# Moving the 80 KB load of the last 64 MLP units from the first to the last of four w_down loads

## The chip, the core and the metric

The kernel runs on one core of one Trainium2 chip. The metric is the device time of one execution in microseconds (us). Times of the trace are counted from the start of the profiled span, which begins after the execution does: a run of 205.6 us has a span of 203.8 us.

The engines are named as the profile does: PE is TensorE's matmul and PEld its weight load, DVE is VectorE, ACT ScalarE, POOL GpSimd, SPq the queue of SyncE, which issues the loads. The page counts 16 DMA engines, and each load of 128 rows leaves 16 increments of its semaphore in the trace (the "landings"), for the last load of before from 198.33 to 200.49 us. The load has *landed* with the sixteenth. The trace doesn't name the engine of an increment; below, each increment is read as one engine's share of the load having arrived, which is the author's reading.

## The reference

One decode step: layer norm, attention over a cache of 4,096 keys for 32 heads, a residual, layer norm, and a gated MLP with 1,728 hidden units. Only its last product matters here.

```python
def _B_ref(x, w_gate, w_up, w_down):        # x: 640, w_gate and w_up: 640 x 1728
    g = jnp.einsum("bsd,df->bsf", x, w_gate)
    u = jnp.einsum("bsd,df->bsf", x, w_up)
    h = _gelu(g) * u
    return jnp.einsum("bsf,fd->bsd", h, w_down)   # w_down: 1728 x 640
# ... attention left out
h2 = h + _B_ref(_layernorm(h), w_gate, w_up, w_down)
```

## The kernel before

Nearly everything that the kernel reads is read once, 84 MB, over one queue: wq, then K and V of eight groups of four heads, parts of wo between them, then w_gate, w_up and w_down. 1,728 hidden units are 13 columns of 128 (unit `p * 13 + c` is row p of column c) and 64 more. The 64 rows of w_down left over are loaded as 128 half rows of 320 values (640 bytes), so that they fill 128 partitions too. They make columns 13 and 14 of `hid`, the hidden units that w_down multiplies: one for the left halves and one for the right.

The loads of w_down wait for the buffer of a K tile, and there are four of them:

```python
WD = ((0, 8), (8, 11), (11, 13))       # columns of the three large loads
FULL, NFC, YR, YW = 13, 15, 4, 160
# ...
load("wg", wg_sb, ...)                 # w_gate, 2,160 KB
load("wu", wu_sb, ...)                 # w_up, 2,160 KB
SP.wait_ge(S["pe"], pe_at(NQ - SLOTS, ("s", 1)))
load("wd0", wd_last, B_w_down[FULL * P : DF, :].rearrange("i (b d) -> (i b) d", b=PER))   # 80 KB
wd_rows = B_w_down[0 : FULL * P, :].rearrange("(p c) d -> p c d", c=FULL)
for i, (a, b) in enumerate(WD):        # 1,280, 480 and 320 KB
    load(f"wd{i + 1}", wd_sb[:, a:b, :], wd_rows[:, a:b, :])
```

The output row of 640 values is kept as four rows of 160, one for each 32-column group of the array. A column of `hid` is the stationary operand, 128 x 1. So a column of w_down takes four matmuls, one in each column group, and these run side by side: in the trace of before, the last eight begin within 0.01 us of each other in each set of four, and the second set 0.07 us after the first (200.61 after 200.54 us). Below, such a set of four is called a *pass*. Columns 13 and 14 take two matmuls each and are one pass together.

```python
end("u", up(u_ps, wu_sb, "wu"))
fill(4)                                 # matmuls without use
PE.wait_ge(S["dve"], D_HID)             # hid is ready
down = {FULL: "wd0", 0: "wd1", WD[1][0]: "wd2", WD[2][0]: "wd3"}
order = [*range(WD[0][1]), *range(FULL, NFC), *range(WD[0][1], FULL)]
for c in order:
    if c in down:
        landed_once(down[c])            # PE waits for the load
    for r in range(YR):
        if c < FULL:
            w = wd_sb[:, c, r * YW : (r + 1) * YW]
        elif r // 2 == c - FULL:
            w = wd_last[:, (r % 2) * YW : (r % 2 + 1) * YW]
        else:
            continue
        inst = y_matmul(r, slice(0, YW), hid[:, c : c + 1], w, c == order[-1])
end("y", inst)
# ... VectorE waits for that, adds h_row and SyncE stores y_row
```

`hid` is the end of a chain through all engines: the last scores, Exp, P times V, the projection, layer norm, gate, gelu, up.

The softmax here doesn't subtract the row's maximum and nothing guards it: scores larger than these inputs give would overflow.

## Time and profile before

| | before |
|---|---|
| time, median of 3 runs | 205.67 us (205.64 to 205.74) |
| profiled run, span | 205.61 us, 203.8 us |
| DMA, mean over the span | 414 GB/s, 84.38 MB |
| last load of w_down landed | 200.49 us |
| VectorE's last addition began | 200.90 us |

The first view is the page of the kernel before. The two rows have a digit for each of 40 slices of the span: the busy share of the DMA engines in tenths, and what they moved.

```profile
DMA  7999999999999999999999999999999999999991
GB/s 249 402 468 418 389 482 412 415 434 444 447 404 414 447 421 424 431 431 450 418 424 416 452 424 431 444 437 424 424 431 437 412 418 457 431 404 429 430 388 47
```

The DMA engines are busy throughout, except in the first and the last slice. The next view is the end of the chain of waits that ended last, in order of time (start, duration, what).

```profile
167.43 33.07 DMA big<-in_B_w_down_dram
200.49 0.04 issue
200.54 0.34 PE tp_105 L455 x8
200.88 0.02 issue
200.90 0.33 DVE y_row L725
```

The last load, of columns 11 and 12, is issued at 167.4 and lands at 200.49 us, 33 us later; eight loads issued before it, 13.9 MB, land in that time. Eight matmuls follow, which are two passes, and VectorE starts 0.41 us after the landing. The timeline of the same stretch (start, duration, engine, line, operation; in brackets the idle time before it and what ended it) shows when TensorE could begin.

```profile
198.59 0.18 DVE L723 TENSOR_TENSOR hid<-g_sb,u_col 128x15 bf16<-128x15 f32 x1
198.83 0.58 PEld L455 LDWEIGHTS tp_105<-big,hid 128*1 128x1 bf16 x36 [0.54 <-DVE hid L723]
...
199.75 0.17 PEld L455 LDWEIGHTS tp_105<-big,hid 128*1 128x1 bf16 x12 [0.34 <-DMA big<-in_B_w_down_dram]
200.54 0.10 PEld L455 LDWEIGHTS tp_105<-big,hid 128*1 128x1 bf16 x8 [0.62 <-DMA big<-in_B_w_down_dram]
200.54 0.31 PE L455 MATMUL tp_105<-big,hid 128*1 128x160 bf16 x8 [0.41 <-DMA big<-in_B_w_down_dram]
200.90 0.33 DVE L725 TENSOR_TENSOR y_row<-tp_105,h_row 128x160 bf16<-128x160 f32 x1 [2.12 <-PE tp_105 L455]
```

The first 36 matmuls wait for `hid`, the last 20 for loads. In this trace the four loads land in the order of issue, at 195.45, 198.55, 199.71 and 200.49 us.

### The profile page before, as it was taken

How to read it: one execution, taken by the hardware profiler on the slowest of the kernel's cores; microseconds unless marked ns; L12 is line 12 of the kernel's file. 1: busy time of each engine (PE TensorE's matmuls, PEld its weight loads, DVE VectorE, ACT ScalarE, POOL GpSimd, SP SyncE). 2: the span in 40 equal slices, each digit the busy share in tenths (PEclk: the TensorE clock that was granted, in tenths of full speed). 3: DMA queues.
4: the chain of work that ended last, by engine and by line, in shares of the span. 5: the costliest groups of instructions: out<-in, count | busy, mean ns of one | idle time of the engine just before them, and what ended most of it. 6: DMA issues, size and time to landing. Idle time of an engine off the chain costs nothing. (4 is left out here: it accounts for less than half of the span.)

```text
span 203.8 us, 7455 instructions
## 1 busy us (share of the span) xinstructions
PE 149.6 (73%) x3451; PEld 136.6 (67%) x3453; DVE 70.6 (35%) x163; ACT 81.5 (40%) x179; POOL 20.3 (10%) x20
## 2 busy tenths in 40 slices
PE   0003679765995499849984998389839989988993
PEld 0001179665995499849974997389839989987431
DVE  4003138201560067005700670039005801842460
ACT  0000327530566047704770467028703862773000
POOL 8301000710000001700000017000000000000000
PEclk9999969955698569856985698569856985995799
DMA  7999999999999999999999999999999999999991
GB/s 249 402 468 418 389 482 412 415 434 444 447 404 414 447 421 424 431 431 450 418 424 416 452 424 431 444 437 424 424 431 437 412 418 457 431 404 429 430 388 47
DMA packets 4058, 84.38 MB, mean 414 GB/s; under 512 B 464, under 2 KB 592, under 8 KB 848
## 3 DMA queue, kind: packets, MB, share of 16 engines
q1 hardware_dynamic: 4048, 84.23, 96.9%
q8 instruction: 8, 0.13, 0.3%
q14 instruction: 2, 0.02, 0.0%
HBM read 84.23 MB, written 0.00 MB: 413 GB/s over the span
## 5 line engine op out<-in xcount | busy, mean ns | idle before, releaser
L281 PE MATMUL o<-ex,big 128*128 128x4 bf16 x1024 | 29.8, 166 | 10.9 <-ACT ex L611 6.5
L281 PEld LDWEIGHTS o<-ex,big 128*128 128x128 bf16 x1024 | 28.4, 103 | 12.2 <-ACT ex L611 7.7
L597 ACT COPY big<-tp_104 128x1024 bf16<-128x1024 bf16 x16 | 16.2, 1012 | 50.0 <-PE tp_104 L255 50.0
L255 PE MATMUL tp_103<-ident,big 128*128 128x128 bf16 x256 | 23.9, 249 | 13.6 <-PEq L180 13.6
L255 PEld LDWEIGHTS tp_103<-ident,big 128*128 128x128 bf16 x256 | 19.5, 115 | 14.0 <-issue 14.0
L624 DVE COPY big<-tp_103 128x1024 bf16<-128x1024 bf16 x24 | 16.5, 688 | 21.2 <-PE tp_103 L255 21.2
L255 PE MATMUL tp_104<-ident,big 128*128 128x128 bf16 x256 | 23.5, 245 | 0.0
L255 PE MATMUL tp_105<-ident,big 128*128 128x128 bf16 x256 | 23.1, 242 | 0.0
L542 POOL COPY wo<-wo_in 128x5120 bf16<-128x5120 bf16 x3 | 13.4, 4451 | 93.5 <-PE a L292 93.5
L255 PE MATMUL tp_106<-ident,big 128*128 128x128 bf16 x256 | 22.5, 239 | 0.0
L255 PEld LDWEIGHTS tp_104<-ident,big 128*128 128x128 bf16 x256 | 19.3, 113 | 0.0
L255 PEld LDWEIGHTS tp_105<-ident,big 128*128 128x128 bf16 x256 | 18.9, 111 | 0.0
L255 PEld LDWEIGHTS tp_106<-ident,big 128*128 128x128 bf16 x256 | 18.6, 109 | 0.0
L624 DVE COPY big<-tp_106 128x1024 bf16<-128x1024 bf16 x24 | 16.6, 691 | 2.9 <-PE tp_106 L255 2.4
L268 PE MATMUL sb<-q_78,big 128*128 128x4 bf16 x512 | 14.2, 164 | 4.5 <-issue 4.5
L597 ACT COPY big<-tp_105 128x1024 bf16<-128x1024 bf16 x16 | 16.2, 1014 | 2.6 <-PE tp_105 L255 2.5
L268 PEld LDWEIGHTS sb<-q_78,big 128*128 128x128 bf16 x512 | 13.6, 96 | 4.6 <-issue 4.6
L611 ACT ACTIVATE ex<-sa 32x64 bf16<-32x64 f32 x32 | 9.8, 307 | 11.4 <-PE sa L268 11.2
L624 DVE COPY big<-tp_105 128x1024 bf16<-128x1024 bf16 x16 | 11.1, 692 | 8.4 <-PE tp_105 L255 8.1
L268 PE MATMUL sa<-q_78,big 128*128 128x4 bf16 x512 | 14.0, 164 | 0.0
L268 PEld LDWEIGHTS sa<-q_78,big 128*128 128x128 bf16 x512 | 13.5, 96 | 0.6
L681 DVE COPY o_raw<-o 128x4 f32<-128x4 f32 x4 | 0.7, 163 | 36.1 <-PE o L281 36.1
(111 smaller groups left out, 115.8 us busy)
## 6 DMA issues: line engine op xcount, KB each, us to landing
big<-in_A_v_cache_dram SPq DMA_DIRECT2D x8, 4096.0 KB, 33.9
big<-in_A_k_cache_dram SPq DMA_DIRECT2D x7, 4096.0 KB, 27.4
big<-in_A_wq_dram SPq DMA_DIRECT2D x1, 5120.0 KB, 15.4
wo_in<-in_A_wo_dram SPq DMA_DIRECT2D x4, 1280.0 KB, 28.3
big<-in_A_k_cache_dram SPq DMA_DIRECT2D x2, 2048.0 KB, 24.3
big<-in_B_w_gate_dram SPq DMA_DIRECT2D x1, 2160.0 KB, 39.5
big<-in_B_w_up_dram SPq DMA_DIRECT2D x1, 2160.0 KB, 44.1
big<-in_B_w_down_dram SPq DMA_DIRECT2D x1, 1280.0 KB, 32.1
```

The source lines that it names most:

```text
L255: inst = PE.transpose(tp_b[g % NBANK][:, b * DH : (b + 1) * DH], kt[slot][:, g * GRP + b, :], ident[:])
L268: inst = PE.matmul(s_ps[half][:, j % (NB // 2), :], lhsT=kt[slot][:, j, :], rhs=q8[:, slot * QH : (slot + 1) * QH], start=True, stop=True,)
L281: inst = PE.matmul(o_ps, lhsT=vt[slot][:, j, :], rhs=e_t[:, j, :], start=(j == 0), stop=(j == NB - 1))
L542: POOL.tensor_copy(wo_t[:], wo_in[:]).then_inc(S["wo"], 1)
L597: ACT.copy(group(m % SLOTS, g), tp_g[g % NBANK]).then_inc(S["act_pe"], 1)
L611: inst = ACT.activation(e_t[r, cols, i], s_ps[half][r, :, i], AF.Exp, scale=SCALE, accum_out=rs_all[r, half, h : h + 1])
L624: DVE.tensor_copy(group(m % SLOTS, g), tp_g[g % NBANK]).then_inc(S["dve_pe"], 1)
L681: event(DVE.tensor_copy(o_raw[:, HG * turn : HG * turn + QH], o_ps))
```

## The change

The intent is to have as little as possible left to do when the last load lands. The total of the loads can't shrink, but the smallest of them, whose columns need only one pass, can come last.

```diff
-    order = [*range(WD[0][1]), *range(FULL, NFC), *range(WD[0][1], FULL)]
+    order = range(NFC)
...
-            inst = y_matmul(r, slice(0, YW), hid[:, c : c + 1], w, c == order[-1])
+            inst = y_matmul(r, slice(0, YW), hid[:, c : c + 1], w, c >= FULL)
...
-    load("wd0", wd_last, B_w_down[FULL * P : DF, :].rearrange("i (b d) -> (i b) d", b=PER))
     wd_rows = B_w_down[0 : FULL * P, :].rearrange("(p c) d -> p c d", c=FULL)
     for i, (a, b) in enumerate(WD):
         load(f"wd{i + 1}", wd_sb[:, a:b, :], wd_rows[:, a:b, :])
+    load("wd0", wd_last, B_w_down[FULL * P : DF, :].rearrange("i (b d) -> (i b) d", b=PER))
```

## The prediction

> **What bounds the kernel.** DMA. The page's slices show the DMA engines at 90% or more of every slice but the first and the last, 414 GB/s on average (84.38 MB in a span of 203.8 us). The chain of waits that ended last is a DMA from 167.43 to 200.49 us (w_down's columns 11 and 12, the last load), then 8 matmuls on the y bank (from 200.54), the final addition on VectorE at 200.90, and the store. The other engines are off this chain: `hid` is ready at 198.8, and TensorE then waits three times for w_down (y's weight loads 1.0 us in two waits, the matmuls 0.4 us).
>
> **What the change does.** It removes and adds no work: 84 MB, 56 down matmuls and four loads stay. It moves the 80 KB load (128 rows of 640 B) behind the other three. [...] the four loads land in the order of issue, at 195.45, 198.55, 199.70 and 200.49 us. The moved load's packets took 32 ns each (the last load's 2,560 B took 102), so with 8 on each engine it is about 0.26 us of each engine's queue; it landed 0.19 us after w_up. So I expect the three large loads 0.19 to 0.26 us earlier, at about 198.3, 199.5 and 200.3, and the small one last at about 200.49, unchanged, because every engine has the same packets to move in total. From the last packet's end to the landing is 0.44 us for the small load and for the large last one alike, so no gain or loss there.
>
> **What lies on the critical path.** Only what follows the last landing. Before, 8 matmuls (two columns times four column groups): VectorE starts 0.36 us after the first. After, 4 matmuls, one for each column group: one pass of the array instead of two. I estimate 0.08 us less (8 matmuls spanned 0.31 us, one alone 0.23). The earlier landings are worth nothing: columns 0 to 7 still wait for `hid` at 198.83, columns 8 to 10 then run at about 199.5 to 199.8, columns 11 and 12 start at about 200.3 and are through TensorE's queue before 200.5.
>
> **Predicted time.** 205.67 - 0.08 = 205.59 us; range 205.35 to 205.82, since the DMA engines finish up to 2.2 us apart (first and last engine of the last load: 198.33 and 200.49), and a stalled packet on the slowest (two of 3,840 B took 355 and 414 ns instead of 149) is larger than the effect. Faster by over 2%: 0.005; within 2%: 0.99; slower: 0.005.
>
> **What would show it.** Right: in the landings, the large loads 0.2 us earlier and the last one still 33 us after its issue; in the timeline, a last group of 4 y matmuls instead of 8, and VectorE 0.25 to 0.3 us after its start instead of 0.36; all before 198 us unchanged. Wrong step "same last landing": the small load lands later than 200.49 by more than 0.1 us. Wrong step "second pass": VectorE still starts 0.36 us after the last group's start.
>
> **What would make it wrong.** Small packets at the end of the queue may not overlap as they do amid large ones, so that the slowest engine ends later and the gain is lost or turned round (about +0.2 us); or the last loads may spread differently over the engines and end earlier or later together.

"8 on each engine" and "the same packets" for every engine are the author's estimate, from 128 packets of 640 bytes and 16 engines; the trace doesn't name the engine of a packet. Both traces have 4,048 packets in this queue. That small packets overlap amid large ones is read from the same numbers: eight of 32 ns are 0.26 us, and the load landed 0.19 us after w_up.

## The result

| | before | after |
|---|---|---|
| time, median of 6 runs each | 205.65 us (205.54 to 205.74) | 205.50 us (205.37 to 205.74) |
| ratio | | 0.9993, 95% interval 0.998 to 1.0006 |
| last load of w_down landed | 200.49 us | 200.51 us |
| `hid` written, start | 198.59 us | 199.31 us |
| VectorE's last addition began | 200.90 us | 200.84 us |

A ratio is the mean time of one kernel's runs over that of the other's of the same rounds, so it is not quite the ratio of the medians in the table. Executions over 1.5% slower than the fastest of the same kernel are left out of the means. The interval holds 1: the time is the same within what six runs can tell, and the median lies in the predicted range.

The landings of the profile after are 198.34, 199.51, 200.30 and 200.51 us: the large loads 0.2 us earlier, the last one where it was. The timeline of the kernel after, for the same stretch as shown of before:

```profile
199.31 0.18 DVE L723 TENSOR_TENSOR hid<-g_sb,u_col 128x15 bf16<-128x15 f32 x1
199.55 1.09 PEld L455 LDWEIGHTS tp_105<-big,hid 128*1 128x1 bf16 x56 [0.54 <-DVE hid L723]
199.55 1.24 PE L455 MATMUL tp_105<-big,hid 128*1 128x160 bf16 x56
200.84 0.32 DVE L725 TENSOR_TENSOR y_row<-tp_105,h_row 128x160 bf16<-128x160 f32 x1 [1.35 <-PE tp_105 L455]
```

This isn't what had been expected. `hid` is 0.72 us later than in the profile before, so all 56 matmuls appear as one group with no wait, and the chain of waits of this kernel contains no DMA at all:

```profile
196.54 2.02 PE tp_104 L482 x40
198.59 0.69 DVE u_col L685
199.55 1.27 PE tp_105 L455 x56
200.84 0.32 DVE y_row L725
```

Read by itself, this chain says that the kernel is now bound by TensorE. The timeline, asked for a narrow window from 200.45 us on, says something else:

```profile
200.55 0.09 PEld L455 LDWEIGHTS tp_105<-big,hid 128*1 128x1 bf16 x4
200.84 0.32 DVE L725 TENSOR_TENSOR y_row<-tp_105,h_row 128x160 bf16<-128x160 f32 x1 [1.35 <-PE tp_105 L455]
```

The last four weight loads start at 200.55 us, 0.04 us after the last landing, just as the last eight did before (200.54 after 200.49). The matmuls still at work hid that wait from the view. So the DMA ended last here too, and VectorE started 0.33 us after the landing instead of 0.41. But it was close.

Why was `hid` late? The change touches nothing before it. At 152.8 us the two executions are level within 0.02 us (the first transposes of a K tile). The scores of the seventh group of heads start at 162.72 us before and 163.19 after, those of the last group at 179.17 and 179.89. So all of the delay, 0.72 us, is there 20 us before the end, and from there to `hid` nothing is added to it. What differs in between is when TensorE's granted clock was 0.5 instead of 1.0. In the trace of before, each set of eight transposes took 0.85 us between 153.8 and 156.4 us, at 0.50, and 0.45 us between 157.2 and 158.9 us, at 1.00. Here are two rows of a table by stretches (busy time by engine, then PEclk, the granted clock; then DMA), first before, then after:

```profile
156.00:160.00 4.00, 4.00 (x68) 4.00 (x66) 3.56 (x10) 2.44 (x3) 0.00 (x0) 0.92 0.97 418
172.00:176.00 4.00, 4.00 (x60) 4.00 (x59) 2.55 (x5) 2.56 (x3) 0.00 (x0) 0.79 0.99 426
```

```profile
156.00:160.00 4.00, 4.00 (x60) 4.00 (x58) 3.15 (x8) 2.05 (x3) 0.00 (x0) 0.79 1.00 430
172.00:176.00 4.00, 4.00 (x52) 4.00 (x50) 2.45 (x4) 1.83 (x2) 0.00 (x0) 0.66 1.03 442
```

TensorE is busy for all of these rows in both, but at the lower clock it gets through fewer matmuls (60 instead of 68, and 52 instead of 60). The first row goes with 0.47 us of delay, the second with 0.25. A third stretch of half clock follows, and its end tells how far apart the two executions are in the phase of the clock, that is in where the half-clock stretches lie. The row from 190 to 192 us, before and after:

```profile
190.00:192.00 2.00, 1.97 (x23) 0.85 (x16) 0.96 (x3) 0.00 (x0) 0.00 (x0) 0.81 1.03 441
```

```profile
190.00:192.00 2.00, 2.00 (x35) 1.27 (x36) 0.67 (x2) 0.00 (x0) 0.00 (x0) 0.56 1.01 432
```

The clock records of both traces hold no values but 0.5 and 1.0. So a mean of 0.81 over these 2 us puts the end of the half-clock stretch at 190.76 us, and a mean of 0.56 at 191.76 us. This last stretch is 6.83 us long in both. Most changes of clock in the records lie 10.24 us apart (the others 3.41, 6.83 or 13.65), and from 40 us on the same changes come 1.0 us later in after than in before. What sets their time isn't shown.

So there were three things to test: that passes after the last landing are what the order of loads decides; that the last landing stays where it is; and that a second chain, the compute chain through `hid`, ends so near to the DMA's end that the clock's phase decides which is last.

### The profile page after: what moved, and what is told of

It reads as the page before. It is cut to its first block, busy times and chain, and to the rows that moved or that the text cites. A ratio compares the mean times of both kernels' runs of the same rounds, so it can differ in the third digit from the quotient of the medians.

```text
span 203.8 us, 7457 instructions
## 1 busy us (share of the span) xinstructions
PE 152.3 (75%) x3453; PEld 139.1 (68%) x3453; DVE 70.6 (35%) x163; ACT 81.6 (40%) x179; POOL 20.3 (10%) x20
## 3 DMA queue, kind: packets, MB, share of 16 engines
q1 hardware_dynamic: 4048, 84.23, 96.8%
## 5 line engine op out<-in xcount | busy, mean ns | idle before, releaser
L255 PE MATMUL tp_103<-ident,big 128*128 128x128 bf16 x256 | 24.9, 255 | 10.9 <-PEq L180 10.9
L255 PEld LDWEIGHTS tp_103<-ident,big 128*128 128x128 bf16 x256 | 20.4, 118 | 11.4 <-issue 11.4
L255 PE MATMUL tp_104<-ident,big 128*128 128x128 bf16 x256 | 24.1, 249 | 0.0
L255 PE MATMUL tp_105<-ident,big 128*128 128x128 bf16 x256 | 23.3, 244 | 0.0
L255 PE MATMUL tp_106<-ident,big 128*128 128x128 bf16 x256 | 23.1, 242 | 0.0
L255 PEld LDWEIGHTS tp_104<-ident,big 128*128 128x128 bf16 x256 | 19.9, 115 | 0.0
L255 PEld LDWEIGHTS tp_105<-ident,big 128*128 128x128 bf16 x256 | 19.2, 112 | 0.0
L255 PEld LDWEIGHTS tp_106<-ident,big 128*128 128x128 bf16 x256 | 18.9, 111 | 0.0
```

What stands on the lines that cost most here:

```text
L255: inst = PE.transpose(tp_b[g % NBANK][:, b * DH : (b + 1) * DH], kt[slot][:, g * GRP + b, :], ident[:])
```

## The experiments

All ran on the same program otherwise, and all gave correct results except where it is said. In the first set, an extra load holds back only the w_down loads, so that `hid` can't be last. Its data are read by nothing:

```diff
+    PADW = 25 * DH
+    pad_sb = part(FULL * D + HALVES, PADW)
...
     PE.wait_ge(S["dve"], D_HID)
+    landed_once("pad")
...
     SP.wait_ge(S["pe"], pe_at(NQ - SLOTS, ("s", 1)))
+    load("pad", pad_sb, A_k_cache[0, 0, 0 : 25 * P, :].rearrange("(p j) d -> p (j d)", p=P))
```

### pad_before and pad_after: the change with hid out of the way

> An extra load of 0.82 MB ahead of the w_down loads, so that the last landing comes about 2.0 us later (at about 202.5 us) and hid (198.8 to 199.6 us) can never be last; result still correct. Theory (fixed last landing, then one pass of about 0.08 us for each column that is left): about 207.65 us, VectorE's last addition starts about 0.41 us after the last landing (8 matmuls, two passes). Rivals give the same here; it is the base of the other padded runs.

> The whole change, with the same extra load. Theory: last landing as in pad_before to within 0.1 us, VectorE starts about 0.33 us after it (4 matmuls, one pass), so 0.08 us less than pad_before. Rival 'fixed latency' (matmuls after the landing overlap, only their latency counts): again 0.41, same time. Rival 'small packets last are costly': last landing 0.1 us or more later than in pad_before, no gain or a loss.

Measured: pad_before 207.50 us (207.33 to 207.65), pad_after 207.43 us (207.37 to 207.50), five runs each. The timelines, pad_before first, show what is left after the last landing, which is at 202.36 and at 202.43 us.

```profile
202.40 0.10 PEld L457 LDWEIGHTS tp<-big,hid 128*1 128x1 bf16 x8 [0.62 <-DMA big<-in_B_w_down_dram]
202.77 0.33 DVE L729 TENSOR_TENSOR y_row<-tp,h_row 128x160 bf16<-128x160 f32 x1 [3.49 <-PE tp L457]
```

```profile
202.47 0.09 PEld L457 LDWEIGHTS tp<-big,hid 128*1 128x1 bf16 x4
202.77 0.33 DVE L729 TENSOR_TENSOR y_row<-tp,h_row 128x160 bf16<-128x160 f32 x1 [3.74 <-PE tp L457]
```

VectorE starts 0.41 us after the landing with two passes and 0.34 us after it with one, so the pass is worth 0.07 us. In this pair of profiles the landing itself was 0.07 us later, so VectorE started at the same time in both. The change of the median, 0.07 us, is of the expected size and sign, but the runs of the two kernels overlap. With the five runs each of pad_before2 and pad_after2 (below, on other chips) the means of ten are 207.52 and 207.41 us, 0.10 us apart with a standard error of 0.03.

### pad_pe_only and pad_load_only: one half of the change each

> Only TensorE's order is changed (columns 0 to 14 in turn); the loads stay as before, small one first, columns 11 and 12 last. So 12 matmuls (3 passes) follow the last landing. Theory: VectorE 0.49 us after it, 0.08 us more than pad_before. Rival 'fixed latency': 0.41.

> Only the load is moved to the end; TensorE keeps the old order, so it waits for the small load before columns 8 to 12, and 24 matmuls (6 passes) follow the last landing. Theory: last landing as in pad_after, VectorE about 0.73 us after it, 0.32 us more than pad_before in the time. Rival 'fixed latency': 0.41, no difference.

In pad_pe_only the load stays first and only `order = range(NFC)` (with its stop flag) is taken from the change, so that three passes follow the last landing. In pad_load_only the load is moved and the old order of columns is kept, so that six do. Measured: 207.55 us (207.50 to 207.69, 5 runs) and 207.87 us (207.66 to 208.07, 4 runs). The end of the chain of waits of pad_load_only:

```profile
167.96 34.48 DMA big<-in_B_w_down_dram
202.44 0.04 issue
202.49 0.62 PE tp L457 x24
203.10 0.02 issue
203.13 0.33 DVE y_row L729
```

VectorE starts 0.69 us after the landing here (0.73 expected), and in pad_pe_only 0.48 us (0.49 expected). The rival, by which only the latency of the last matmul counts and 4 matmuls cost what 24 do, falls. Either half of the change alone leaves more work after the landing than pad_before has. In the time, pad_load_only is clearly slower (0.37 us in the median, no run in common); pad_pe_only, at 0.05 us, can't be told from pad_before.

### last8: the largest load last, without the extra load

```diff
-    for i, (a, b) in enumerate(WD):
-        load(f"wd{i + 1}", ...)
+    for i in (1, 2, 0):
+        a, b = WD[i]
+        load(f"wd{i + 1}", ...)
...
+    order = [*range(FULL, NFC), *range(WD[0][1], FULL), *range(WD[0][1])]
```

> No extra load; the order of loads is small one, columns 8 to 10, 11 and 12, then the large load of columns 0 to 7, TensorE in that order: 32 matmuls (8 passes) follow the last landing. Theory: last landing at 200.4 to 200.6 as ever, VectorE about 0.83 to 0.89 us after it (six passes of 0.07 to 0.08 more than before's 0.41), and no longer hidden by hid even where it is late: 0.35 to 0.5 us slower than before. Rival 'the order of loads doesn't matter': same as before.

Measured: 205.95 us (205.89 to 206.15) against 205.66 us of before in the same rounds, ratio 1.0014 (1.0001 to 1.0027). The last landing is at 200.43 us, as ever:

```profile
200.43 0.04 issue
200.47 0.75 PE tp L455 x32
201.22 0.02 issue
201.25 0.33 DVE y_row L726
```

VectorE starts 0.82 us after it. The gap of the medians, 0.29 us, is less than expected, since before's own median contains executions that ended late for another reason (below); its fastest run, 205.44 us, is 0.45 us under last8's fastest.

All profiles together, by what followed the last landing:

| passes after the last landing | VectorE's start minus last landing, us | runs |
|---|---|---|
| 1 | 0.33 to 0.34 | after, after_again, after_fill2, pad_after, pad_after2 |
| 2 | 0.41 | before, pad_before, pad_before2 |
| 3 | 0.48 | pad_pe_only |
| 6 | 0.69 | pad_load_only |
| 8 | 0.82 | last8 |

From one pass to eight is 0.48 us for seven passes, that is 0.07 us each.

### after_again and nowd: the second chain

> The changed kernel once more, on the chip of the next three runs. Theory: two chains end within some 0.7 us of each other, the last landing (about 200.5 us) and hid, which is ready between 198.8 and 199.6 us according to where the half-clock stretches of TensorE fall; only where the first ends last does the change give its 0.08 us. About 205.5 us; 0.03 to 0.08 less than before.

> No w_down load at all (the down matmuls read what lies in the buffer, so the result is wrong on purpose): the compute chain alone. Theory of two nearly tied chains: VectorE's last addition starts 1.29 us after hid, so at 200.1 to 200.9 us, the time is only 0.1 to 0.5 us under the changed kernel's, and scatters more than with the extra load. Rival 'loads alone bound the end': 0.7 us less or more in every run.

nowd has no w_down loads; its result is wrong (relative error 0.049).

```diff
-        if c in down:
-            landed_once(down[c])
...
-    SP.wait_ge(S["pe"], pe_at(NQ - SLOTS, ("s", 1)))
-    for i, (a, b) in enumerate(WD):
-        load(f"wd{i + 1}", wd_sb[:, a:b, :], wd_rows[:, a:b, :])
-    load("wd0", wd_last, ...)
```

Measured in the same rounds:

| | runs, us |
|---|---|
| before | 205.44, 205.45, 205.55, 205.56, 205.61, 205.66, 205.70, 205.81, 205.98, 206.04, 206.07 |
| after_again | 205.50, 205.57, 205.58, 205.87, 205.96, 205.98 |
| nowd | 204.40, 204.58, 204.86, 205.17, 205.19, 206.21 |

The changed kernel is no faster than before in these rounds (ratio 1.0005, 0.9992 to 1.0017), although its profile (205.58 us) again shows VectorE 0.33 us after the last landing. And without any of the four loads, which took 5.2 us from w_up's landing to the last, the kernel is 0.65 us faster than before in the median and slower in one run. Against after_again, for which the expectation was put, it is 0.72 us: more than the 0.1 to 0.5 us expected, and as much as the rival "loads alone bound the end" wanted. But the rival wanted that in every run, and only three of the six are so much faster than before's median; the runs lie from 1.3 us below it to 0.5 us above. So the rival falls by the scatter and not by the median, and the gap between the two chains was put too small.

The end of nowd's chain of waits, and its row from 190 to 192 us:

```profile
197.50 0.69 DVE u_col L679
198.46 1.17 PE tp L455 x56
199.65 0.33 DVE y_row L719
```

```profile
190.00:192.00 2.00, 1.94 (x16) 0.67 (x8) 1.21 (x5) 0.00 (x0) 0.00 (x0) 0.92 0.99 423
```

This was nowd's fastest run, 204.40 us. The half clock ended at 190.3 us by that row, and the down product could start at 198.46 us. In four profiles without the extra load the two go together: half clock until 190.3, 190.8, 191.6 and 191.8 us; down product from 198.46 (nowd), 198.83 (before), 199.33 (after_again) and 199.55 us (after).

The other traces extend this and limit it. In eleven of the fourteen the fillers are the same and the last half-clock stretch is 6.83 us long. Its end lies between 190.32 us (nowd) and 192.36 (pad_eight), the write of `hid` starts between 198.22 and 199.73 us in the same order, and always 19.40 to 19.44 us after the first scores of the last group of heads. So the scatter of `hid` is made before those scores. In pad_pe_only and after_eight the last stretch is 10.24 us long and ends at 193.3 and 193.1 us, yet `hid` starts at 198.96 and 198.84: the end of that stretch alone doesn't tell when `hid` comes.

Is it this chain that makes some runs of before late? The padded kernels speak for it. They have 2 us more of DMA and the same compute, so that only a late compute chain is hidden. Their 25 runs with one to three passes lie within 207.33 to 207.69 us. The 38 runs of before lie within 205.44 to 206.22 us, 11 of them over 205.8. No late execution of before was profiled, so which wait came last in those 11 is argued and not shown. An estimate says that it could be `hid`: nowd takes 1.43 us from the start of `hid`'s write to VectorE's last addition, so the latest `hid` of the traces, 199.73 us, would put that addition at 201.16 us, 0.26 us later than in the profile before. The mean granted clock is lower in the 11 late runs than in the other 27 (0.787 and 0.794 in the mean), but the two overlap. No run sets the clock's phase, so that it drives `hid` rests on the traces above.

### after_fill2: fewer fillers

```diff
     end("g", up(g_ps, wg_sb, "wg"))
-    fill(5)
+    fill(2)
     end("u", up(u_ps, wu_sb, "wu"))
```

> The changed kernel with 2 instead of 5 filler matmuls between the gate and the up product, which made up start 0.5 us (profile before) or 1.3 us (after) after its weights had landed. Theory: hid comes at most 0.1 us earlier, as VectorE's gelu chain ends only 0.1 us before up's end; time within 0.1 us of the changed kernel, less rather than more. If it is 0.3 us or more less, the fillers and not VectorE bound the compute chain.

Measured: 205.64 us (205.30 to 205.88), after_again 205.73 us. The down product started at 199.18 us, 0.15 us earlier than in after_again with nearly the same clock phase: the up product now ends before VectorE's gelu chain does, and VectorE decides. A hair more than the 0.1 us expected; in the time nothing that these runs can tell.

### pad_eight, pad_after2 and after_eight: a try for a faster end

In the traces so far the 16 DMA engines finish the last load 1.8 to 2.2 us apart, and the slowest decides; the first eight land 0.4 to 2.2 us ahead of it (the expectation below says 0.2 to 2.1). The skew is made in the first 70 us and then stays: it is 1.38 us for wq and about 2.16 us from 80 us on in before. If the last load used only engines that run ahead, the last landing could come earlier. That a load of 8 rows uses 8 engines was the author's premise.

```diff
-    load("wd0", wd_last, ...)
+    last_rows = B_w_down[FULL * P : DF, :].rearrange("i (b d) -> (i b) d", b=PER)
+    for i in range(0, P, 8):
+        load("wd0", wd_last[i : i + 8, :], last_rows[i : i + 8, :])
...
-        PE.wait_ge(S[name], 16)
+        PE.wait_ge(S[name], 256 if name == "wd0" else 16)
```

> A try for a faster end, with the extra load: the small load, last in the queue, is cut into 16 loads of 8 rows[...]. In every trace so far 8 engines landed the last load 0.2 to 2.1 us ahead of the slowest, and the skew was there long before. If the 8 engines used are the early half, the last landing is that of columns 11 and 12 (0.2 us earlier than with the small load on all 16) and the time is 0.2 us less than pad_after2; if they are the late half, the last landing is about 0.26 us later, and the time too. Rival 'the rate of the whole, not the slowest engine, sets the end': no difference.

> The padded changed kernel again, for comparison on the same chip: about 207.45 us, VectorE 0.33 to 0.34 us after the last landing.

> The same cut of the small load without the extra load, as a candidate to beat both kernels. Theory: at best 0.2 us less than after (205.3 to 205.5 us), and nothing in executions where hid comes late; if the 8 engines are the late half, 205.7 to 205.9 us.

Measured: pad_eight 210.73 us, pad_after2 207.39 us (207.33 to 207.46), after_eight 208.74 us. Both tries are slower, pad_eight by 3.3 us than pad_after2 and after_eight by 3.1 us than before in the same rounds, which neither theory had foreseen. In pad_eight, the end of the chain of waits:

```profile
190.73 14.76 DMA big<-in_B_w_down_dram
205.49 0.04 issue
205.53 0.27 PE tp L457 x4
205.80 0.02 issue
205.82 0.33 DVE y_row L731
```

The loads were all issued by 190.7 us, and the last data packet of 640 bytes ended at 202.27 us. But the last increment of the semaphore came at 205.49 us, 3.2 us later; in pad_after2 it is 0.48 us. In after_eight, where it is seen best, the increments arrive in groups of eight every 0.2 us. The author's estimate from this spacing is about 0.2 us more for each load, and 16 in a row some 3.2 us; what takes that time isn't shown. Besides 16 increments recorded right after the issues there are 128, 8 for each load, where a load of 128 rows leaves 16. Read as above, each load used 8 engines, but the trace doesn't name them, and whether these eight are the early half remains open. The run has one merit for the theory: the four last matmuls stand alone in it, and VectorE starts 0.29 us after them, against 0.36 us for eight in before.

### pad_before2: does the order shift the last landing?

> The padded kernel with the old order once more. What it is to tell: with the small load last, the last landing came 7.17, 7.29 and 7.33 us after w_up's in the padded traces, with it first 7.18 and 7.18. If the order itself makes the last landing later, this run gives 7.18 again or less. If the scatter is that of one DMA engine held up by a 16 KB instruction fetch, which is last in some executions and not in others, any value from 7.15 to 7.35 can come. VectorE 0.41 us after the last landing in either case; 207.4 to 207.6 us.

Measured: 207.52 us (207.48 to 207.61), VectorE 0.41 us after the last landing, which came 7.18 us after w_up's. So with the extra load, the small load first gave 7.18, 7.18 and 7.18 us, and the small load last 7.17, 7.29 and 7.33 us. Without it, from w_up's landing to the last: 5.23 (before) and 5.27 us (last8) with the small load first; 5.28 (after), 5.42 (after_again) and 5.52 us (after_fill2) with it last.

This points to a last landing that is up to 0.3 us later in some executions of the changed kernel. The landings of the single shares show where that comes from. They don't name the engine, but they can be matched from load to load: in each of these eleven traces one share falls 1.5 to 1.7 us behind the other fifteen, once, and stays there. In before this is from the 1,280 KB load to the next, where every landing moves by about 1.17 us and one by 2.66. The share had been the second to sixth to land, and whether it becomes the last depends on how far ahead it was. It became the last in the four latest traces (after_again, after_fill2, pad_after and pad_load_only), 0.11 to 0.25 us behind the second slowest. Taken at the second slowest, these four give 5.27, 5.28, 7.18 and 7.17 us. So without the late share all traces agree within 0.05 us, whatever the order of loads. A 16 KB instruction fetch of about 1.1 us lies in the packet records of all eleven, at 196.3 to 197.5 us when it starts, which is about when the share falls behind; that it is the reason wasn't isolated.

The late share came last in four of the six traces with the small load last, and in none of the five with it first: why that should go with the order isn't known, and with eleven traces it may be chance. The times of the padded kernels don't show it: 207.49 and 207.54 us in the mean before, 207.43 and 207.39 us after (five runs each, on three chips).

No version beat both kernels by more than these runs can tell.

## Why the prediction was right, point by point

- *DMA bounds the kernel.* Right for the profile before, and in the profile after the last landing was still what the last matmuls waited for. But "the other engines are off this chain" was said of one execution as if it held of all. nowd shows the compute chain alone at 204.40 to 206.21 us.
- *The large loads land 0.19 to 0.26 us earlier, the last landing stays at 200.49 us.* Right: 198.34, 199.51, 200.30 and 200.51 us (expected 198.3, 199.5, 200.3, 200.49). For other executions only within 0.3 us, because one engine's share comes 1.5 to 1.7 us late and is the last in some; without it, within 0.05 us.
- *One pass less, 0.08 us.* Right: 0.33 to 0.34 us instead of 0.41 us from the landing to VectorE, and 0.07 us for each pass over one to eight passes. VectorE started 0.29 us after the last group of weight loads, within the 0.25 to 0.3 us expected.
- *Columns 0 to 7 still wait for `hid` at 198.83 us; all before 198 us unchanged.* This step failed. The down product started at 199.55 us, and the up product 0.71 us later than before, because TensorE's half-clock stretches ended 1.0 us later; the last scores, at 179.89 instead of 179.17 us, had all of that delay. It did no harm to the prediction only because the DMA ended last all the same, by about 0.1 us: with nowd's 1.43 us from `hid` to VectorE's addition, the compute chain alone would have come to it at 200.74 us, and it began at 200.84.
- *205.59 us, range 205.35 to 205.82.* Right: 205.50 us. The agreement to 0.09 us is partly luck. The 0.15 us between the medians is more than the pass can give, and in the later rounds the difference had the other sign; three of the six runs of after_again lie above the range, at 205.87 to 205.98 us. The range was justified with stalled packets and skewed DMA engines; the larger scatter came from executions over 205.8 us, which the padded kernels don't have.

## What to carry to other kernels

When loads fill the queue to the end, as here, look first whether their order moves the last landing (here by no more than 0.05 us, the one late share apart); otherwise it only decides how much work is still to be done after it. Count that work in passes of the array (0.07 us each here), put the load with the fewest passes last, and change both the order of loads and the order of use: here either alone left more passes after the landing (three and six instead of two). Before costing a gain of 0.1 us at the end of one chain, see how far behind the next chain ends and how much that one moves from run to run; a load that nothing reads, put ahead of the last ones, separates the two.
